# Linear attention with two expert layers on one core: norms first, transposes reordered, routing reordered

## The chip, the cores and the metric

One core of one Trainium2 chip. The time is that of the device for one execution, in microseconds (us). The kernel before was run three times: 834.59 us in the median, 834.49 to 839.33.

## What is computed

Attention with a positive feature map, then a top-1 mixture of eight experts, then a dense layer of three matmuls joined by max. All is f32, 2304 tokens of 512 features (4 batches of 576 tokens, 8 heads of 64).

```python
def phi(x):
    proj = np.einsum('bhsd,df->bhsf', x, w_phi)
    proj = proj - np.max(np.abs(proj), axis=-1, keepdims=True)
    return np.concatenate([np.exp(proj), np.exp(-proj)], axis=-1)
q_p, k_p = (phi(q), phi(k))
kv = np.einsum('bhsf,bhsd->bhfd', k_p, v)
z = np.sum(k_p, axis=2)
num = np.einsum('bhsf,bhfd->bhsd', q_p, kv)
den = np.einsum('bhsf,bhf->bhs', q_p, z)[..., None] + 1e-06

xn = x / (np.linalg.norm(x, axis=-1, keepdims=True) + 1e-06)
en = expert_emb / (np.linalg.norm(expert_emb, axis=-1, keepdims=True) + 1e-06)
logits = xn @ en.T / tau
expert_idx = np.argmax(logits, axis=1)
# out[token] = gate * relu(x @ w1[e]) @ w2[e], then max(x @ w1, x @ w2, x @ w3) @ w_out
```

## The kernel before

The order of all instructions is written out by hand; each engine runs its own list in order, and semaphores make it wait for the others. The attention part goes in rounds, `for r in range(R1)` with 18 rounds, numbered from 0. The keys are cut into 18 steps, the queries into 16 pieces that follow the keys by four and more rounds. A round does, in this order:

- `q_front`: the projection of a query piece on TensorE (tiles `psqf`), copied out by ScalarE (`pq`), and its largest magnitude over the partitions by a reduction on GpSimd (`mq`). `q_exp`: for the piece of the round before, the subtraction on VectorE (`pq<-pq,mq`) and two exponentials on ScalarE (`ex`).
- `k_proj(r + 1)`: the projection of the next key step on TensorE into two PSUM banks (`pskp`, j = 0 and 1), for each the largest magnitude (`mk`) and the subtraction (`pk`) on VectorE, and two exponentials on ScalarE (`kp`).
- `fin`, in rounds 5, 9 and 14 and after the loop: what is left to do for a finished batch (transposes `psz` and `pskv`, copies `zp` and `kvb` on VectorE).
- `xwork`: a finished piece of the attention's output x. In rounds 7, 9, 11, 13 and 16 a new piece is begun: transposes of the denominators (`psxd`), their reciprocals (`r`) and the raw logits (`lp`, `lraw`) on VectorE, the transpose of the numerators (`psx`), the scaling (`x`) on VectorE, its write to DRAM (`x_d`), and its sum of squares on ScalarE (`junk`). In the round after each of these the rest of its tiles follow.
- `k_T(r + 2)`: transposes of a later key step (`pskT`), copied by ScalarE (`kT`). `q_T`: transposes of a later query piece (`psqT`), copied by VectorE (`qT`).
- `k_acc`: accumulation of this round's keys and values (`kv`) and of the keys' sums (`z`) in banks of their own; `q_num` and `q_den`: numerators (`psn`, copied to `oT` by ScalarE) and, in every second of these rounds, denominators (`psd`, copied to `dn` by VectorE); `k_pair(r + 1)`: the sum of two key tiles on VectorE (`zr`), in whose place `z` of this round must have been read.

All the transposes and projections take their PSUM bank in turn from one pool of five (`bank`, tag "W"), so each waits until the reader of the tile allocated five earlier has finished.

`prep_experts` computes the norms of the expert embeddings: 8 rows of 512, a square and sum, then a chain of some twenty small operations on VectorE (`rsqrt`) and the scaling of `emb`; its second half transposes them (`ps_en`). The first half stands at the end of round 0, its VectorE part behind `zr` of that round. After the loop come the last numerators, the logits' argmax (`rt.argmax`) and the routing (`rt.blocks`, the generator `chain`): counts per expert (`inc`, `rt_n`), positions (`nb` to `tr`), one-hot groups (`R`) and the matmul that gives each block its token list (`rt_tok`, copied to `s2t`). Between its parts the last five tiles of x (13 to 17) are transposed, scaled and written; their sums of squares end ScalarE's list before the expert layer's weight casts. The expert layer begins with a gather of x by that list on GpSimd (`xs<-x_d,s2t`). Loads of keys, values and queries are issued from SyncE's queue, w_phi, embeddings and tau from ScalarE's.

Of the kernel before, what the change touches and what calls it, by code (L numbers as in the profile page):

```python
# [8 lines left out]
F32 = mybir.dt.float32  # L9
# [37 lines left out]
def attention(tc, q, k, v, w_phi, expert_emb, tau, x_d, lraw, ssq, ident, io, late, rt, ids):  # L47
# [19 lines left out]
    with ExitStack() as ctx:  # L67
# [60 lines left out]
        def load_kv(n):  # L128
            if n < len(loads):
                f, *a = loads[n]  # L130
                f(*a)

        w2 = cp.tile([P, NF], F32, tag="w2", name="w2")
        nc.scalar.dma_start(out=w2[0:D], in_=w_phi)
        load_kv(0)
        nc.scalar.dma_start(out=w2[D:P], in_=w_phi)
        emb = cp.tile([E, H * D], F32, tag="emb", name="emb")
        nc.scalar.dma_start(out=emb, in_=expert_emb)
        taub = cp.tile([E, 1], F32, tag="taub", name="taub")
        nc.scalar.dma_start(out=taub, in_=tau.rearrange("(a b) -> a b", b=1).to_broadcast([E, 1]))  # L140
        load_u(0, 1, (0,))
        load_q(0)
        load_u(0, 1, (1,))
        load_kv(2)
# [20 lines left out]
        rt.prep(QR)  # L165

        def prep_experts():
            sq = wk.tile([P, H * D], BF16, tag="junk", name="esq_junk", bufs=1)
            esq = cp.tile([E, 1], F32, tag="esq", name="esq")
            nc.scalar.activation(sq[0:E], emb, AF.Square, accum_out=esq)  # L170
            ern = cp.tile([E, 1], F32, tag="ern", name="ern")
            for _ in rsqrt(nc, cp, ern, esq, [E, 1], "e"):
                pass
            nc.vector.tensor_tensor(ern, ern, esq, op=ALU.mult)
            nc.vector.tensor_scalar(ern, ern, 1e-6, taub, op0=ALU.add, op1=ALU.mult)
            nc.vector.reciprocal(ern, ern)
            nc.vector.tensor_scalar(emb, emb, ern, None, op0=ALU.mult)
            yield
            ps = bank("ps_en")
            for p in range(NP_):  # L180
                nc.tensor.transpose(ps[:, p * E:(p + 1) * E], emb[:, p * P:(p + 1) * P], ident[:E, :E])
            psv = ps[:, 0:NP_ * E].rearrange("p (a e) -> p a e", e=E)
            nc.vector.tensor_copy(enp[0:D, :, 2:2 + E], psv[0:D])
            nc.vector.tensor_copy(enp[D:P, :, 2 + E:2 + 2 * E], psv[D:P])
            yield


        kT, kp, zr, kvs, acc = {}, {}, {}, {}, {}

        def k_T(n):  # L190

# [11 lines left out]
        def k_proj(n):  # L203
            if n >= NS:
                return
            psb = [bank(f"pskp{n}_{j}").rearrange("p (i f) -> p i f", f=NF) for j in range(2)]
            for i in range(4):
                for j in range(2):
                    x = slice(j * D, (j + 1) * D)
                    nc.tensor.matmul(psb[j][:, i, :], kT[n][x, i, :], w2[x], start=True, stop=True)  # L210
            o = kp[n] = wk.tile([P, 4, 2, 2 * NF], F32, tag="kp", name=f"kp{n}")
            for j in range(2):
                m = wk.tile([P, 4], F32, tag="mk", name=f"mk{n}_{j}")
                nc.vector.tensor_reduce(m, psb[j], axis=AX.X, op=ALU.max, apply_absolute_value=True)
                d = wk.tile([P, 4, NF], F32, tag="pk", name=f"pk{n}_{j}")
                nc.vector.tensor_tensor(d, psb[j], m.unsqueeze(2).to_broadcast([P, 4, NF]), op=ALU.subtract)
                nc.scalar.activation(o[:, :, j, 0:NF], d, AF.Exp)
                nc.scalar.activation(o[:, :, j, NF:], d, AF.Exp, scale=-1.0)


        def k_pair(n):
# [175 lines left out]
        def x_sq(t):  # L397
            junk = wk.tile([P, H * D], BF16, tag="junk", name=f"junk{t}", bufs=1)
            nc.scalar.activation(junk, xs.pop(t).rearrange("p h d -> p (h d)"), AF.Square, accum_out=ssq[:, t:t + 1])
# [52 lines left out]
                    yield  # L452

        R1 = back[NV - 4]
        k_T(0)
        k_T(1)
        k_proj(0)
        k_pair(0)
        pe = prep_experts()
        fin = None  # L460
        for r in range(R1):

# [5 lines left out]
                    q_exp(m * NP_ + 2 * g + pp)  # L468
            k_proj(r + 1)

            if fin is not None:
                for _ in fin:
                    pass
                fin = None
            if xwork:
                if next(xwork[0], "end") == "end":
                    xwork.pop(0)
                    if xwork:
                        next(xwork[0])
            k_T(r + 2)  # L480
            if r + LEAD + 1 in at:
                q_T(at[r + LEAD + 1])
            for _ in pe if r == 2 else ():
                pass

# [23 lines left out]
                    k_acc(*pc)  # L509
            k_pair(r + 1)  # L510
            if r == 0:
                next(pe)
            if r == 7:
                rt.token_ids(ids, QR)
            if r == R1 - 3:
# [21 lines left out]
        for p in range(2, NP_):  # L537
            q_num(m0 * NP_ + p)
        xa = [(t, rv, x_out(t)) for t, rv in ra]
        q_num((m0 + 1) * NP_)  # L540
        free = [("kv0", 512), ("kv1", 512), ("z", 256)]
        chain = rt.blocks(lambda nm: ps1.tile([P, free[0][1]], F32, tag=free.pop(0)[0], name=nm), bank)
        next(chain)
        x_put(*xa[0], act=True, dma=nc.scalar, sq=False)
        for p in range(1, NP_):
            q_num((m0 + 1) * NP_ + p)
            if p == 1:
                x_put(*xa[1], act=True, dma=nc.scalar, sq=False)
        xb = [(t, rv, x_out(t)) for t, rv in rb]
        x_put(*xb[0], act=True, dma=nc.scalar, sq=False)  # L550
        for x in xb[1:]:
# [1 line left out]
            x_put(*x, dma=nc.sync, sq=False)  # L553
        for _ in chain:
            pass
        for t in ta + tb:
            x_sq(t)


# [715 lines left out]
```

## Time and profile before

| | before |
|---|---|
| median of three runs (lowest to highest) | 834.59 us (834.49 to 839.33) |
| the profiled execution: its time, its span | 835.01 us, 833.2 us |
| TensorE busy, share of the span | 790.5 us, 95% |
| VectorE, ScalarE, GpSimd busy | 520.2, 453.4, 163.6 us |
| mean granted clock of TensorE | 0.969 |

The page of the profile gives for each engine its busy time. A stage in which TensorE is busy nearly throughout is bound by it; in one with pauses the rows in order of time tell what released each wait, in brackets: `[1.92 <-DVE pk L216]` means that the engine stood still 1.92 us until VectorE's instruction on line 216 had finished. PE is TensorE, DVE VectorE, ACT ScalarE, POOL GpSimd, SPq SyncE's DMA queue.

### The profile page before, as it was taken

What the parts mean: (1) busy time and instruction counts of PE and PEld (TensorE: products, weight loads), DVE (VectorE), ACT (ScalarE), POOL (GpSimd) and SP (SyncE); (2) the same over time, 40 slices, a digit from 0 to 9 for tenths busy, and PEclk for the clock granted to TensorE, in tenths of its full rate; (3) what the DMA queues carried; (4) which work ended last, traced back from release to release, by engine and by line L of the source; (5) the groups of instructions that cost most, each with busy time, mean ns of one, the idle gap of its engine ahead of it and who ended that gap; (6) DMA issues with size and microseconds to landing.
All of it is one profiled execution on the core that took longest, in us unless ns stands there. A gap on an engine that the chain in (4) does not pass through costs nothing. (4 is left out here: it accounts for less than half of the span.)

```text
span 833.2 us, 14145 instructions
## 1 busy us (share of the span) xinstructions
PE 790.5 (95%) x5617; PEld 661.5 (79%) x5617; DVE 520.2 (62%) x670; ACT 453.4 (54%) x632; POOL 163.6 (20%) x117
## 2 busy tenths in 40 slices
PE   7788988998989999999999999999999999999996
PEld 5655655575578888888888887999989999899984
DVE  5976567456779999989889897899312222122210
ACT  4576556476488888888888795544221112211111
POOL 1554224244052021011061102000121001200001
PEclk8899889789999999999999999999999999999999
DMA  8434323222334427641764542442021001200001
GB/s 208 109 81 105 78 66 83 55 77 79 143 127 147 153 97 285 250 139 43 258 235 176 190 160 103 157 160 102 26 76 52 1 1 39 76 1 1 0 26 52
DMA packets 61989, 87.82 MB, mean 105 GB/s; under 512 B 9488, under 2 KB 39832, under 8 KB 61920
## 3 DMA queue, kind: packets, MB, share of 16 engines
q1 hardware_dynamic: 53248, 64.25, 24.2%
q0 software_dynamic: 4880, 15.99, 5.9%
q10 hardware_dynamic: 3792, 6.64, 2.1%
q8 instruction: 46, 0.75, 0.4%
q14 instruction: 23, 0.19, 0.1%
HBM read 129.59 MB, written 16.00 MB: 175 GB/s over the span
## 5 line engine op out<-in xcount | busy, mean ns | idle before, releaser
L879 DVE TENSOR_TENSOR wL<-raw,wH 128x2048 fp32r<-128x2048 f32 x88 | 199.8, 2288 | 20.0 <-ACT wH L878 19.1
L878 ACT CAST wH<-raw 128x2048 fp32r<-128x2048 f32 x88 | 167.5, 1915 | 28.0 <-PE ph L905 13.7
L1106 PE MATMUL ps<-yH,m2WH 128*128 128x384 f32 x432 | 145.1, 336 | 1.3 <-ACTq L1242 1.3
L1106 PE MATMUL ps<-yH,m2WL 128*128 128x384 f32 x432 | 145.0, 336 | 0.0
L1106 PE MATMUL ps<-yL,m2WH 128*128 128x384 f32 x432 | 145.0, 336 | 0.0
L326 POOL PARTITION_ALL_REDUCE mq<-pq x32 | 70.5, 2252 | 122.3 <-ACT pq L324 122.3
L1106 PEld LDWEIGHTS ps<-yH,m2WH 128*128 128x128 f32 x432 | 81.2, 188 | 1.8 <-ACTq L1242 1.7
L1114 ACT CAST h2H<-mm 128x384 fp32r<-128x384 f32 x36 | 18.5, 514 | 115.6 <-DVE mm L1111 115.6
L1106 PEld LDWEIGHTS ps<-yL,m2WH 128*128 128x128 f32 x432 | 81.2, 188 | 0.1
L1106 PEld LDWEIGHTS ps<-yH,m2WL 128*128 128x128 f32 x432 | 81.2, 188 | 0.0
L849 POOL DMA_INDIRECT xs<-x_d,s2t x22 | 44.9, 2040 | 153.3 <-PE psxT L888 88.5
L1060 POOL DMA_INDIRECT yg<-ys,c2s x18 | 24.8, 1378 | 245.0 <-PE psyT L1075 220.2
L937 PE MATMUL py<-wH,hH 128*128 128x512 f32 x176 | 70.4, 400 | 0.4 <-ACT hH L923 0.4
L937 PE MATMUL py<-wH,hL 128*128 128x512 f32 x176 | 69.1, 393 | 0.3 <-DVE hL L924 0.3
L937 PE MATMUL py<-wL,hH 128*128 128x512 f32 x176 | 68.8, 391 | 0.0
L1110 DVE TENSOR_TENSOR mm<-mm,ps 128x384 f32<-128x384 f32 x36 | 19.9, 553 | 74.4 <-PE ps L1106 74.4
L905 PE MATMUL ph<-wH,xH 128*128 128x512 f32 x176 | 56.5, 402 | 0.7 <-ACT xH L891 0.7
L905 PE MATMUL ph<-wH,xL 128*128 128x512 f32 x176 | 54.8, 392 | 0.1
L905 PE MATMUL ph<-wL,xH 128*128 128x512 f32 x176 | 54.5, 391 | 0.0
L1111 DVE TENSOR_TENSOR mm<-mm,ps 128x384 f32<-128x384 f32 x36 | 20.0, 555 | 43.7 <-PE ps L1106 43.7
L1128 ACT ACTIVATE ot<-pso,gatec 128x512 f32<-128x512 f32 x18 | 12.4, 689 | 60.2 <-PE pso L1126 32.9
L1129 POOL DMA_INDIRECT out_dram<-ot,c2t x18 | 17.7, 983 | 132.3 <-ACT ot L1128 129.6
(214 smaller groups left out, 1446.7 us busy)
## 6 DMA issues: line engine op xcount, KB each, us to landing
raw<-in_moe_w_dram SPq DMA_DIRECT2D x88, 1024.0 KB
wr<-in_moe_w_dram SPq DMA_DIRECT2D x18, 512.0 KB
ys<-y ACTq DMA_DIRECT2D x22, 256.0 KB
q<-in_q_dram SPq DMA_DIRECT2D x8, 576.0 KB
kv<-in_v_dram SPq DMA_DIRECT2D x8, 512.0 KB
x_d<-x SPq DMA_DIRECT2D x15, 256.0 KB
kv<-in_k_dram SPq DMA_DIRECT2D x7, 512.0 KB
wr<-in_moe_w_out_dram SPq DMA_DIRECT2D x6, 512.0 KB
```

Of the source, the lines that this page charges most:

```text
L326: nc.gpsimd.partition_all_reduce(mx.rearrange("p a b -> p (a b)"), d.rearrange("p a b -> p (a b)"), P, ReduceOp.absmax)
L849: nc.gpsimd.indirect_dma_start(out=d, out_offset=None, in_=self.x_d, in_offset=bass.IndirectOffsetOnAxis(ap=self.s2t[:, j:j + 1], axis=0))
L878: nc.scalar.copy(wH, ex.raw[i])
L879: nc.vector.tensor_tensor(wL, ex.raw[i], wH.bitcast(F32), op=ALU.subtract)
L905: nc.tensor.matmul(ph[:, n * 512:(n + 1) * 512], a[:, cs], w[:, c * DF + n * 512:c * DF + (n + 1) * 512], start=(kc == 0 and f == 0), stop ...
L937: nc.tensor.matmul(py, a[:, cs], w[:, ws], start=(fc == 0 and q == 0), stop=(fc == 7 and q == 2))
L1060: self.nc.gpsimd.indirect_dma_start(out=d, out_offset=None, in_=self.ys[0:rows, :], in_offset=bass.IndirectOffsetOnAxis(ap=self.rt.c2s[:, ...
L1106: nc.tensor.matmul(ps, w[:, c], y[:, k], start=(k == 0 and q == 0), stop=(k == NK - 1 and q == 2))
L1110: nc.vector.tensor_tensor(m, m, pss[1], op=ALU.max)
L1111: nc.vector.tensor_tensor(m, m, pss[2], op=ALU.max)
L1114: nc.scalar.copy(hH[:, f], m)
L1129: nc.gpsimd.indirect_dma_start(out=self.out, out_offset=bass.IndirectOffsetOnAxis(ap=self.rt.c2t[:, t:t + 1], axis=0), in_=o, in_offset=None)
```

## The change

At the start: the embeddings are loaded ahead of w_phi on ScalarE's queue; the keys of the second unit are loaded ahead of the values of the first; the norms of the embeddings are taken on VectorE altogether (square and sum instead of ScalarE's) and stand ahead of the first key step. In round 0 the query transposes stand at the round's end. In the rounds: `k_proj` is cut into the projection and `k_exp`, the two halves of the key exponentials; `k_T` and `q_T` stand right behind the projection, `q_T`'s copies between the two halves, and `fin` and `xwork` behind all of these. At the end: the routing's first part stands ahead of the second query half's numerators, its second part ahead of the last three x tiles; tile 13 is scaled by VectorE instead of ScalarE; and the sums of squares of tiles 13 and 14 stand between the copies of numerators.

```diff
+        emb = cp.tile([E, H * D], F32, tag="emb", name="emb")
+        nc.scalar.dma_start(out=emb, in_=expert_emb)
         w2 = cp.tile([P, NF], F32, tag="w2", name="w2")
         nc.scalar.dma_start(out=w2[0:D], in_=w_phi)
-        load_kv(0)
         nc.scalar.dma_start(out=w2[D:P], in_=w_phi)
-        emb = cp.tile([E, H * D], F32, tag="emb", name="emb")
-        nc.scalar.dma_start(out=emb, in_=expert_emb)
...
+        load_u(0, 0, (0,))
         load_u(0, 1, (0,))
+        load_u(0, 0, (1,))
         load_q(0)
...
-            sq = wk.tile([P, H * D], BF16, tag="junk", name="esq_junk", bufs=1)
+            sq = wk.tile([P, H * D], F32, tag="x", name="esq_junk", bufs=5)
+            nc.vector.tensor_tensor(sq[0:E], emb, emb, op=ALU.mult)
             esq = cp.tile([E, 1], F32, tag="esq", name="esq")
-            nc.scalar.activation(sq[0:E], emb, AF.Square, accum_out=esq)
+            nc.vector.tensor_reduce(esq, sq[0:E], axis=AX.X, op=ALU.add)
...
+            kpb[n] = psb
+
+        def k_exp(n):
+
+            if n >= NS:
+                return
+            psb = kpb.pop(n)
             o = kp[n] = wk.tile([P, 4, 2, 2 * NF], F32, tag="kp", name=f"kp{n}")
             for j in range(2):
...
                 nc.scalar.activation(o[:, :, j, NF:], d, AF.Exp, scale=-1.0)
+                if j == 0:
+                    yield
...
+        pe = prep_experts()
+        next(pe)
         k_T(0)
         k_T(1)
         k_proj(0)
+        for _ in k_exp(0):
+            pass
         k_pair(0)
-        pe = prep_experts()
...
             k_proj(r + 1)
 
+            k_T(r + 2)
+            ke = k_exp(r + 1)
+            next(ke, None)
+            if r and r + LEAD + 1 in at:
+                q_T(at[r + LEAD + 1])
+            for _ in ke:
+                pass
             if fin is not None:
...
-            k_T(r + 2)
-            if r + LEAD + 1 in at:
-                q_T(at[r + LEAD + 1])
             for _ in pe if r == 2 else ():
...
             if r == 0:
-                next(pe)
+                q_T(at[LEAD + 1])
...
         xa = [(t, rv, x_out(t)) for t, rv in ra]
-        q_num((m0 + 1) * NP_)
         free = [("kv0", 512), ("kv1", 512), ("z", 256)]
         chain = rt.blocks(lambda nm: ps1.tile([P, free[0][1]], F32, tag=free.pop(0)[0], name=nm), bank)
         next(chain)
-        x_put(*xa[0], act=True, dma=nc.scalar, sq=False)
-        for p in range(1, NP_):
+        x_put(*xa[0], dma=nc.sync, sq=False)
+        x_put(*xa[1], act=True, dma=nc.scalar, sq=False)
+        for p in range(NP_):
             q_num((m0 + 1) * NP_ + p)
-            if p == 1:
-                x_put(*xa[1], act=True, dma=nc.scalar, sq=False)
+            if p < 2:
+                x_sq(ta[p])
+        next(chain)
...
-        for t in ta + tb:
+        for t in tb:
             x_sq(t)
```

What stands where, at three places. VectorE at the start, the kernel before: behind the second key tile come the query copies, the pair sum of round 0 and then the norms (`rs_` and `ern` are the tiles of the chain, `esq` the sums of squares).

```order
L308 COPY qT_237<-psqT_0_238 128x4x72
L308 COPY qT_237<-psqT_1_244 128x4x72
L225 TENSOR_TENSOR zr_273<-kp_215 128x1024
L36 TENSOR_SCALAR rs_ge<-esq 8x1
L37 TENSOR_SCALAR rs_ie<-rs_ge 8x1
L38 TENSOR_SCALAR ern<-rs_ie 8x1
```

The changed kernel, VectorE right behind the identity matrix:

```order
L28 TENSOR_SCALAR ident<-idn 32x32 x4
L170 TENSOR_TENSOR esq_junk<-emb 8x512
L172 TENSOR_REDUCE esq<-esq_junk 8x1
L36 TENSOR_SCALAR rs_ge<-esq 8x1
L37 TENSOR_SCALAR rs_ie<-rs_ge 8x1
L38 TENSOR_SCALAR ern<-rs_ie 8x1
```

The whole chain, with a square and a sum of its own, now stands ahead of the first `mk`, and nothing of it is left behind `zr`.

TensorE in round 7, behind the key projection, before:

```order
L377 MATMUL psxd_1064<-ident,dn_990 128x128 x2
L394 MATMUL psx_1074<-ident,oT_843 128x128 x4
L199 MATMUL pskT_1084<-ident,kv_0_588 128x128 x4
L306 MATMUL psqT_0_1092<-ident,q_651 128x72 x4
L306 MATMUL psqT_1_1098<-ident,q_651 128x72 x4
L253 MATMUL kv_0_699<-kp_906,kv_1_386 32x256 x16
```

and changed:

```order
L201 MATMUL pskT_1052<-ident,kv_0_589 128x128 x4
L317 MATMUL psqT_0_1067<-ident,q_646 128x72 x4
L317 MATMUL psqT_1_1073<-ident,q_646 128x72 x4
L388 MATMUL psxd_1085<-ident,dn_991 128x128 x2
L405 MATMUL psx_1095<-ident,oT_844 128x128 x4
L264 MATMUL kv_0_700<-kp_914,kv_1_387 32x256 x16
```

The transposes of x have moved from ahead of those of keys and queries to behind them; the accumulation `kv` stays last. VectorE in the same round, behind the subtractions of the queries, before:

```order
L214 TENSOR_REDUCE mk_0_1052<-pskp_0_1041 128x4
L216 TENSOR_TENSOR pk_0_1054<-pskp_0_1041,mk_0_1052 128x512
L214 TENSOR_REDUCE mk_1_1058<-pskp_1_1042 128x4
L216 TENSOR_TENSOR pk_1_1060<-pskp_1_1042,mk_1_1058 128x512
L380 TENSOR_SCALAR r_1067<-psxd_1064 128x16
L381 RECIPROCAL r_1067<-r_1067 128x16
L384 TENSOR_TENSOR lp_1070<-psxd_1064,r_1067 128x2x32 x2
L386 TENSOR_REDUCE lraw<-lp_1070 128x16
L407 TENSOR_TENSOR x_1079<-psx_1074,r_1067 128x512
L308 COPY qT_1091<-psqT_0_1092 128x4x72
L308 COPY qT_1091<-psqT_1_1098 128x4x72
```

and changed:

```order
L223 TENSOR_REDUCE mk_0_1060<-pskp_0_1042 128x4
L225 TENSOR_TENSOR pk_0_1062<-pskp_0_1042,mk_0_1060 128x512
L319 COPY qT_1066<-psqT_0_1067 128x4x72
L319 COPY qT_1066<-psqT_1_1073 128x4x72
L223 TENSOR_REDUCE mk_1_1079<-pskp_1_1043 128x4
L225 TENSOR_TENSOR pk_1_1081<-pskp_1_1043,mk_1_1079 128x512
L391 TENSOR_SCALAR r_1088<-psxd_1085 128x16
L392 RECIPROCAL r_1088<-r_1088 128x16
L395 TENSOR_TENSOR lp_1091<-psxd_1085,r_1088 128x2x32 x2
L397 TENSOR_REDUCE lraw<-lp_1091 128x16
L418 TENSOR_TENSOR x_1100<-psx_1095,r_1088 128x512
```

The two query copies have moved from the end to between the first and the second half of the keys.

ScalarE in the routing, from the first x tile that it scales there, before (tile 13, then 14):

```order
L405 ACTIVATE x_2736<-psx_2710,r_2665 128x64 x8
L408 DMA x_d<-x_2736 128x512
L354 COPY oT_2139<-psn_2746 128x288
L405 ACTIVATE x_2756<-psx_2715,r_2665 128x64 x8
L408 DMA x_d<-x_2756 128x512
L354 COPY oT_2139<-psn_2766 128x288
L354 COPY oT_2139<-psn_2776 128x288
L405 ACTIVATE x_2801<-psx_2786,r_2676 128x64 x8
L408 DMA x_d<-x_2801 128x512
L399 ACTIVATE junk_2879,ssq<-x_2736 128x512
L399 ACTIVATE junk_2881,ssq<-x_2756 128x512
```

and changed (tile 14 first):

```order
L416 ACTIVATE x_2730<-psx_2716,r_2666 128x64 x8
L419 DMA x_d<-x_2730 128x512
L365 COPY oT_2140<-psn_2740 128x288
L410 ACTIVATE junk_2750,ssq<-x_2727 128x512
L365 COPY oT_2140<-psn_2752 128x288
L410 ACTIVATE junk_2762,ssq<-x_2730 128x512
L365 COPY oT_2140<-psn_2764 128x288
L365 COPY oT_2140<-psn_2774 128x288
L416 ACTIVATE x_2828<-psx_2813,r_2677 128x64 x8
L419 DMA x_d<-x_2828 128x512
L410 ACTIVATE junk_2877,ssq<-x_2828 128x512
```

One scaling of eight pieces is gone from the list, and two of the five sums of squares (`junk`) stand between the copies; three are left at the end.

## Rows read from the trace of the kernel before

**Rows 1.** Stretches: us, busy us (instructions) of PE, PEld, DVE, ACT, POOL; clock, DMA share, GB/s.

```profile
56.00:211.00 155.00, 141.11 (x1804) 93.59 (x1796) 94.05 (x181) 94.71 (x207) 53.11 (x24) 0.89 0.29 80
260.00:520.00 260.00, 258.88 (x1277) 214.64 (x1275) 238.06 (x179) 215.26 (x175) 47.86 (x25) 1.00 0.50 177
```

**Rows 2.** In order of time, the start: start us, us, engine line op, [idle before <-releaser].

```profile
4.08 1.92 SPq L105 DMA_DIRECT2D q<-in_q_dram  x1
...
7.96 0.69 DVE L214 TENSOR_REDUCE mk<-pskp 128x4 f32<-128x512 f32 x1 [5.10 <-PE pskp L210]
...
16.36 0.61 ACT L218 ACTIVATE kp<-pk 128x512 f32<-128x512 f32 x1
...
18.89 1.25 PE L320 MATMUL psqf<-qT,w 64*128 64x144 f32 x16
19.11 1.23 DVE L225 TENSOR_TENSOR zr<-kp 128x1024 f32<-128x1024 f32 x1 [2.60 <-PE z L258]
```

**Rows 3.** In order of time, the norms' chain in round 1 and round 2's query projection.

```profile
20.26 0.13 DVE L36 TENSOR_SCALAR rs_ge<-esq 8x1 f32<-8x1 f32 x1
...
20.52 4.30 POOL L326 PARTITION_ALL_REDUCE mq<-pq  x2 [6.64 <-ACT pq L324]
...
20.78 1.04 DVE L40 TENSOR_TENSOR rs_te<-ern 8x1 f32<-8x1 f32 x1
...
25.75 0.67 DVE L214 TENSOR_REDUCE mk<-pskp 128x4 f32<-128x512 f32 x1
...
29.25 2.29 PE L320 MATMUL psqf<-qT,w 64*128 64x144 f32 x16 [4.57 <-DVE qT L308]
...
29.68 1.23 DVE L225 TENSOR_TENSOR zr<-kp 128x1024 f32<-128x1024 f32 x1 [0.48 <-ACT kp L218]
```

**Rows 4.** In order of time, round 4: the finished batch's sums.

```profile
52.81 1.02 PE L269 MATMUL z<-kvT,enp 128*32 128x256 f32 x8 [1.39 <-ACT kvT L265]
```

**Rows 5.** In order of time, round 7, in which a piece of x begins.

```profile
82.12 0.44 PE L306 MATMUL psqT<-ident,q 72*128 72x72 f32 x4 [1.92 <-DVE pk L216]
...
82.61 0.69 DVE L216 TENSOR_TENSOR pk<-pskp,mk 128x512 f32<-128x512 f32 x1
...
83.45 0.71 PE L306 MATMUL psqT<-ident,q 72*128 72x72 f32 x4 [0.88 <-DVE r L380]
...
84.09 3.64 PE L253 MATMUL kv<-kp,kv 128*32 128x256 f32 x32
...
85.00 0.81 DVE L308 COPY qT<-psqT 128x288 f32<-128x288 f32 x2
```

**Rows 6.** In order of time, the same places in rounds 5 and 16.

```profile
62.58 1.93 PE L253 MATMUL kv<-kp,kv 128*32 128x256 f32 x32
...
194.53 0.44 PE L306 MATMUL psqT<-ident,q 72*128 72x72 f32 x4 [2.11 <-DVE pk L216]
194.90 3.34 PE L253 MATMUL kv<-kp,kv 128*32 128x256 f32 x32
```

**Rows 7.** Stretches, columns as in rows 1: a pause and two stretches after pauses.

```profile
84.00:88.00 4.00, 4.00 (x42) 1.85 (x44) 1.78 (x5) 1.68 (x4) 0.00 (x0) 0.50 0.21 72
154.00:156.00 2.00, 0.93 (x13) 0.69 (x15) 1.83 (x6) 2.00 (x5) 2.00 (x2) 1.00 0.00 0
159.00:170.00 11.00, 11.00 (x97) 6.23 (x89) 2.89 (x4) 2.97 (x8) 1.72 (x1) 0.50 0.25 58
```

**Rows 8.** In order of time, the routing and the first gather.

```profile
223.79 0.17 DVE L671 TENSOR_SCALAR nb<-rt_n 128x8 f32<-128x8 f32 x1 [1.22 <-PE rt_n L665]
...
230.70 0.95 DVE L628 TENSOR_TENSOR R<-ir,trb 128x768 fp32r<-128x768 f32 x1
...
234.04 0.18 DVE L696 CAST s2t<-rt_tok 128x25 int32<-128x25 f32 x1 [0.28 <-PE rt_tok L685]
...
234.77 0.63 ACT L399 ACTIVATE junk<-x 128x512 bf16<-128x512 f32 x1
...
236.38 1.30 POOL L849 DMA_INDIRECT xs<-x_d,s2t  x1 [29.63 <-ACT junk L399]
```

More of the change, by code (lines that the diff above doesn't have):

```diff
@@ L185, in prep_experts @@
             yield
-        kT, kp, zr, kvs, acc = {}, {}, {}, {}, {}
+        kT, kp, kpb, zr, kvs, acc = {}, {}, {}, {}, {}, {}
         def k_T(n):
```

## The prediction

> **What bounds the kernel now.** I read the table of stretches first [rows 1]. From 260 to 520 us the reader should see TensorE busy 258.88 of 260 us at a granted clock of 1.00: this is the expert layer and the beginning of the dense one, which the change does not touch, and it starts when the routing hands it its first rows. So whatever the attention part and the routing gain or lose reaches the end almost 1:1. Between 56 and 211 us the same table shows TensorE busy 141.11 of 155 us and a clock of 0.89: there are pauses, and the clock is lowered. Here alone can the change act. So I read next the instructions in order of time, at three places: the first rounds [rows 2 to 4], a round in which a new piece of x is begun [rows 5], and the routing [rows 8]. In each, what matters is the releaser in brackets: it says what ended the wait.
>
> Durations are from the profiled execution: span 833.2 us, 835.0 us with what lies around it. The median of the three runs is 834.59, so I use 835.0 as the base and the difference of 0.4 is far below all terms.
>
> **The start.** Today VectorE runs the embeddings' norms in round 1, from 20.26 to 25.75 [rows 3], and only then reduces the keys' projection. The query copies come behind that, and TensorE waits 4.57 us for them until 29.25 [rows 3]. Moved ahead of the keys, the chain fills time in which VectorE waits: it sat idle 5.10 us before its first reduction at 7.96 [rows 2]. How long is it there? Of its 5.5 us two small operations on 8x1 took over 1 us (one stands in [rows 3], 1.04) where the one before took 0.13; they began while partition reductions ran on GpSimd (two from 20.52, 4.30 together). Without GpSimd I count 0.9 less for each: 3.7. To this come a square and a reduction over 8x512, which no row shows on VectorE; bounds are 0 and the 0.69 of the 128x512 reduction [rows 2]; I take 0.65 each, since its row has as many elements in a partition. Sum 5.0. It starts when the embeddings have landed. They now go first on ScalarE's queue, where w_phi went first, and the query load stood behind that until 4.08 [rows 2]. So 4.0 to 9.0, and the first key reduction comes at about 9.1 instead of 7.96: 1.1 late. If the embeddings land only at 6, it is 3 late.
>
> The Trainium skill (SBUF — State Buffer, Who interferes with whom) says that a VectorE operation with two SBUF inputs and a GpSimd operation that reads SBUF exclude one another until the first has finished. By that each of the two would have waited for up to a whole reduction of 2.15, the chain alone would be some 2.6 us shorter than I count and the start 1.1 us better than below, 837.3 in all; the row shows a wait of 0.9 and the sum goes by it.
>
> From the first reduction at 7.96 to the last exponential of the second key tile, 16.36 + 0.61 [rows 2], is 9.0 us of VectorE and ScalarE alone. From 9.1 that gives 18.1. Then the pair sum (1.23 [rows 2]) and the query copy, now behind it (0.81 [rows 5]), so round 1's first query projection starts at 20.1 instead of 18.89 [rows 2]. The reordered loads are hidden: the second key load needs only to be there by then. From 18.89 to the start of the pause (29.25 - 4.57 = 24.7) TensorE needs 5.8 us. Round 2 therefore starts at 25.9 instead of 29.25: **3.3 us gained**.
>
> Some of it is given back at once. The pair sum waits for ScalarE's exponentials of the second half of the keys; today the query copy (0.81) lies between and only 0.48 of wait is left [rows 3]. With the copy moved ahead, nothing lies between: 0.81 more in each of the rounds 1 and 2, where VectorE is what TensorE waits for, and about 0.3 in round 4, where ScalarE's copy of the sums ends a wait of 1.39 [rows 4]. 3.3 - 1.6 - 0.3 = **1.4 us gained** at the end of round 4; bounds 0 and 3.3.
>
> **The x rounds.** There are five rotating PSUM banks, and a transpose takes the bank used five allocations earlier. Counting them after the two banks of the key projection: today the x pieces and the key transpose take the three free banks, and the two query transposes wait for the projection's banks. That is what [rows 5] show: the first at 82.12 released by pk, the second at 83.45, just after the last pk (82.61 + 0.69 = 83.30). After the change key and query transposes take the free banks, and the x transposes (in rounds 5, 9, 14 first those of the finished sums) wait for the same two. The wait is not removed; it changes its owner. The accumulation behind it (84.09) is still held until the last pk, and this pk is now later by the query copies put ahead of it, 0.81 [rows 5]. What lies between release and accumulation is the same: one transposition group. **0.8 us lost** in rounds 5, 7, 11 and 13 each (in round 5 the accumulation stands at 62.58 now [rows 6]), and between 0 and 0.8 in 9 and 14, where two groups more stand behind the wait in either order; I take 0.5. In rounds 10, 12 and 16 only the first pk is needed, which does not move; round 16 shows it (194.53 [rows 6]): nothing. Sum 4 x 0.8 + 2 x 0.5 = 4.2; bounds 2.1 and 5.
>
> **The routing.** The first gather stands at 236.38, 1.0 after ScalarE's last sum of squares (234.77 + 0.63), while its index list was ready at 234.04 + 0.18 [rows 8]. Five such sums end the stage; two now go between the copies, where ScalarE waits anyway, and one ScalarE scaling goes to VectorE. Three remain. The list comes about 0.4 earlier, since the count no longer stands behind a numerator (nb on VectorE at 223.79 [rows 8]). The last x tile is scaled about 1 us later, behind one more one-hot group (0.95 us [rows 8]), so its sum of squares and its write come later too. The gather then comes **1.1 us** earlier; bounds 0.3 and 1.5.
>
> **The clock.** In the rows TensorE's clock falls to 0.50 after pauses: 0.50 at 84 to 88 after the pauses of 1.92 and 0.88 in [rows 5]; and after 154 to 156, where it is busy 0.93 of 2 us, 0.50 for 11 us [rows 7]. Its price is in one pair of rows: the 32 accumulations of a round took 1.93 at 62.58 [rows 6] and 3.64 at 84.09 [rows 5], so 1.7 more. The x rounds' pauses get longer (in round 7 1.92 + 0.88 today, 0.8 more then), and rounds 4, 5 and 14, which have short ones, get pauses near 2. I count one more fall: 1.7 lost; bounds 0 and five falls.
>
> Sum: 835.0 - 1.4 + 4.2 - 1.1 + 1.7 = **838.4 us**, 0.4% slower, which is within what can be told: I take 1% as what a measurement of this kernel distinguishes from no change (its three runs lie between 834.49 and 839.33).
>
> **The rivals.** (A) Faster: a lowered clock ends at a moment of its own, so accumulation that starts later runs less of its time at half speed, and each 0.8 costs 0.4; no new fall comes, and the start keeps its whole 3.3. For it speaks that TensorE is busy all of 84 to 88 and of 159 to 170 while the clock stays low [rows 7]: work alone does not at once end it. 835.0 - 3.3 + 2.1 - 1.1 = 832.7. The Trainium skill (TensorE: Matmul & The Clock Gate, The HAM clock gate) says that the clock is set by a monitor that runs on without regard to the kernel's start; by that rule this rival's first condition holds. If also the 11 us at 0.50 in [rows 7] did not come back, 5 or 6 us more would go: 827. (B) Slower by over 1%: five more falls of the clock, one each in rounds 4, 5, 7, 11, 14. 835.0 - 1.4 + 4.2 - 1.1 + 5 x 1.7 = 845.2. It decides from a pause of 1.9 us on (1.92 in [rows 5], 2.11 in [rows 6], both followed by accumulations of 3.3 to 3.6 us), while the 1.39 in [rows 4] is followed by no fall in the rounds I read; I reckon the new pauses at 1.85. (C) The start gains nothing, because the embeddings land late: 838.4 + 1.4 = 839.8, inside the likeliest case's own range.
>
> **How the numbers follow.** Likeliest case with (C) 0.52, its own range 835 to 842.5; (A) 0.29, of it 0.10 for the 827, whose spread of a few us puts 0.07 below 826.2; (B) 0.17; the rest lies beyond. The range leaves out the far ends of (A) and (B): 829.5 to 845.5. Faster by over 1% (below 826.2) needs that far end of (A): 0.07. Slower by over 1% (above 842.9) is (B) nearly whole: 0.15. Within 1%: 0.78.
>
> **What would show it.** In the profile after: the first key reduction near 9.1 and round 2's query projection near 25.9, without a wait for the query copies; in round 7 the x transposes, not the query's, released by pk, and the accumulation 0.8 later after the last denominator copy than today; two sums of squares between the last output copies and the gather 1.1 earlier after the end of round 17. I am wrong if the accumulations in the x rounds start as early as today or earlier, if the lowered stretches are fewer than today's, or if the first reduction comes later than 11.

## The result, and the profile after

The changed kernel takes 823.84 us in the median (822.45 to 825.75) beside 834.54 (833.85 to 839.33) before: ratio 0.9865, 95% interval 0.9828 to 0.9901. A second comparison gave 823.23 and a ratio of 0.9838 (0.9755 to 0.9922). By the first that is 1.3% faster, by its interval 1.0 to 1.7%; the forecast was 838.4, 0.4% slower, from 829.5 to 845.5.

The profiled execution has a span of 821.5 us (823.43 us in all) and a mean granted clock of 0.986, against 833.2 and 0.969. Its stretches, with the columns of [rows 1]:

```profile
56.00:211.00 155.00, 140.65 (x1958) 92.72 (x1946) 104.60 (x215) 99.88 (x221) 53.11 (x24) 0.98 0.32 90
260.00:520.00 260.00, 256.97 (x1277) 214.84 (x1276) 233.62 (x173) 210.41 (x174) 44.43 (x24) 1.00 0.49 171
```

In the first stretch TensorE is busy as long as in [rows 1], but gets through 154 more matmuls, and the clock column says 0.98 instead of 0.89 (1.00 is the full 2.4 GHz, 0.50 the lower of its two levels, 1.2 GHz). To see where the time went I cut the span at four landmarks: the first query projection (`psqf`) of round 5, the first denominators (`psd`) behind the loop, the first matmul of the expert layer (`ph`), the end.

| us | before | after | difference | forecast |
|---|---|---|---|---|
| start to round 5 | 56.48 | 56.83 | +0.35 | -1.4 |
| round 5 to the end of the rounds | 155.27 | 143.25 | -12.02 | +4.2 and +1.7 |
| routing, to the first `ph` | 29.82 | 28.69 | -1.13 | -1.1 |
| expert and dense layers | 591.63 | 592.73 | +1.10 | 0 |

All of the gain, and all of the error, lies in the second line. The two rows for it, the kernel before and then the changed one:

```profile
56.48:211.75 155.27, 141.38 (x1802) 94.10 (x1798) 94.32 (x182) 94.71 (x207) 53.11 (x24) 0.89 0.29 82
```

```profile
56.83:200.08 143.25, 129.59 (x1801) 87.16 (x1797) 94.16 (x182) 94.33 (x207) 53.11 (x24) 0.98 0.32 88
```

The same 1,801 or so matmuls, 11.8 us less of busy TensorE: the pauses in it are as long in sum as before (13.7 us, and 13.9 before). What changed most is how fast it ran between them. Round 7 of the changed kernel, in order of time (columns as in [rows 5], which answer to it):

```profile
81.56 0.69 DVE L225 TENSOR_TENSOR pk<-pskp,mk 128x512 f32<-128x512 f32 x1
...
82.12 0.57 ACT L203 COPY kT<-pskT 128x512 f32<-128x512 f32 x1
...
82.40 0.41 PE L388 MATMUL psxd<-ident,dn 128*128 128x128 f32 x2 [2.07 <-DVE pk L225]
82.74 0.66 PE L405 MATMUL psx<-ident,oT 128*128 128x128 f32 x4
...
83.33 1.93 PE L264 MATMUL kv<-kp,kv 128*32 128x256 f32 x32
...
83.61 0.69 DVE L225 TENSOR_TENSOR pk<-pskp,mk 128x512 f32<-128x512 f32 x1
```

There is one pause instead of two. `psxd` waits for the first `pk` (81.56 + 0.69), as forecast; but `psx` does not wait for the last `pk`: it runs at 82.74, before that one even starts at 83.61. It comes just behind the end of ScalarE's key copy, 82.12 + 0.57 = 82.69. So the accumulation comes 6.57 us after the round's first query projection (83.33 - 76.76) instead of 7.60 (84.09 in [rows 5], less 76.49), 1.0 earlier where I had forecast 0.8 later; and its 32 matmuls take 1.93 us, not 3.64. The clock, in the stretches of [rows 7] and in two that are low now:

```profile
84.00:88.00 4.00, 4.00 (x70) 2.25 (x64) 3.90 (x10) 2.46 (x6) 0.00 (x0) 1.00 0.18 68
126.00:128.00 2.00, 1.87 (x10) 1.21 (x14) 1.97 (x5) 1.53 (x4) 1.01 (x1) 0.50 0.00 0
...
159.00:170.00 11.00, 9.97 (x135) 7.31 (x134) 8.78 (x20) 8.30 (x21) 4.15 (x3) 1.00 0.41 141
184.00:186.00 2.00, 2.00 (x24) 0.99 (x20) 1.90 (x7) 1.15 (x2) 0.00 (x0) 0.50 0.03 8
```

Rounds 7, 9, 11, 13 and 16 were each followed by a stretch at 0.50 before; now only 11 and 16 are, and the second profile of the changed kernel (after_again, below) shows the same two. I call lost clock the time in a stretch times one less the granted clock: added up over stretches of 1 us it is 17.1 us in the rounds of before and 3.4 in those of after.

The start (the rows that answer to [rows 2] and [rows 3]):

```profile
2.89 0.68 DVE L170 TENSOR_TENSOR esq_junk<-emb 8x512 f32<-8x512 f32 x1
...
8.08 0.20 DVE L177 TENSOR_SCALAR ern<-ern,taub 8x1 f32<-8x1 f32 x1 [0.92 <-DMA taub<-in_moe_tau_dram]
...
8.90 0.67 DVE L223 TENSOR_REDUCE mk<-pskp 128x4 f32<-128x512 f32 x1
...
20.03 2.29 PE L331 MATMUL psqf<-qT,w 64*128 64x144 f32 x16 [3.52 <-DVE qT L319]
...
27.13 1.25 PE L331 MATMUL psqf<-qT,w 64*128 64x144 f32 x16
...
33.65 0.54 PE L183 MATMUL ps_en<-ident,emb 8*128 8x8 f32 x4 [2.58 <-DVE pk L225]
34.12 3.38 PE L264 MATMUL kv<-kp,kv 128*32 128x256 f32 x32
...
37.86 1.25 PE L331 MATMUL psqf<-qT,w 64*128 64x144 f32 x16
...
46.76 1.16 PE L212 MATMUL pskp<-w,kT 64*128 64x128 f32 x14 [0.98 <-ACT pq L335]
```

The chain ends where forecast (first key reduction 9.1 forecast, 8.90 measured; round 1's query projection 20.1 and 20.03), but that projection then runs at the low clock, 2.29 us instead of the 1.25 in [rows 2], and round 2 starts at 27.13, not 25.9. The last four rows show where the rest of the lead goes. In round 2 the transposes of the embeddings (`ps_en`) wait 2.58 us for `pk`. The accumulation behind them still starts 1.27 earlier than before, but takes 3.38 at the low clock, and round 3 begins at 37.86 instead of 37.69. Before, the same accumulation ran at full speed:

```profile
35.39 1.93 PE L253 MATMUL kv<-kp,kv 128*32 128x256 f32 x32
```

In round 4, which begins at 43.97 instead of 45.12, the key projection waits 0.98 for ScalarE's copy of the query projection (`pq`), for which it did not wait before; by its end the lead is gone. The same wait of 0.98 stands in after_fill (below), where the clock is at 1.00 in this round, so the clock does not make it.

The routing (the rows that answer to [rows 8]):

```profile
220.87 0.16 DVE L715 CAST s2t<-rt_tok 128x25 int32<-128x25 f32 x1
...
221.35 0.63 ACT L410 ACTIVATE junk<-x 128x512 bf16<-128x512 f32 x1
...
223.52 1.30 POOL L868 DMA_INDIRECT xs<-x_d,s2t  x1 [28.44 <-issue]
```

The gather stands 23.44 after the end of the rounds (223.52 - 200.08) instead of 24.63: 1.2 earlier, 1.1 forecast. In the expert layer 1.1 is given back. Up to 454 us TensorE keeps its lead there of 12.8 us; from 461.60 on the lead is 11.5 to 11.7. What lies between is a weight cast (`wH`) that waits 2.06 for its load, where before the same cast waited 0.80 for TensorE, and behind it, by the same 1.3 late, the activation `h`, for which the transposes `pshT` wait. The kernel before, then the changed one:

```profile
460.45 1.91 ACT L878 CAST wH<-raw 128x2048 fp32r<-128x2048 f32 x1 [0.80 <-PE py L937]
...
473.10 1.09 PE L919 MATMUL pshT<-ident,h 128*128 128x128 f32 x8
```

```profile
448.94 1.91 ACT L897 CAST wH<-raw 128x2048 fp32r<-128x2048 f32 x1 [2.06 <-DMA raw<-in_moe_w_dram]
...
461.60 1.09 PE L938 MATMUL pshT<-ident,h 128*128 128x128 f32 x8 [1.24 <-ACT h L931]
```

The changed kernel's second profile shows both waits too (2.11 and 1.28). No run tests why the load is late there.

### The profile page after: what moved, and what is told of

Read it like the earlier page. It is cut to its first block, busy times and chain, and to the rows that moved or that the text cites. A ratio compares the mean times of both kernels' runs of the same rounds, so it can differ in the third digit from the quotient of the medians.

```text
span 821.5 us, 14129 instructions
## 1 busy us (share of the span) xinstructions
PE 780.2 (95%) x5617; PEld 655.3 (80%) x5617; DVE 520.5 (63%) x673; ACT 450.2 (55%) x622; POOL 162.6 (20%) x117
## 3 DMA queue, kind: packets, MB, share of 16 engines
q10 hardware_dynamic: 3648, 6.38, 2.1%
## 5 line engine op out<-in xcount | busy, mean ns | idle before, releaser
L868 POOL DMA_INDIRECT xs<-x_d,s2t x22 | 42.3, 1923 | 153.5 <-PE psxT L907 90.1
```

The costliest lines, as they stand in the source:

```text
L868: nc.gpsimd.indirect_dma_start(out=d, out_offset=None, in_=self.x_d, in_offset=bass.IndirectOffsetOnAxis(ap=self.s2t[:, j:j + 1], axis=0))
```

## The experiments

Two theories stood against each other. **The banks** (theory 1 in the expectations): my step on the x rounds failed because the five PSUM banks are not handed out in turn, and what helped is that nothing waits for the last `pk`. **The clock** (theory 5): what helped is that TensorE's clock falls less often; the wait itself is small. Each kernel was compared with runs of before on its own chip; before had medians of 834.5 to 838.2 us there.

| kernel | median us | ratio to before (95%) |
|---|---|---|
| changed | 823.84 | 0.9865 (0.9828 to 0.9901) |
| rounds_only | 828.2 | 0.9914 (0.9877 to 0.995) |
| start_tail | 834.5 | 0.9962 (0.9935 to 0.9989) |
| after_strict | 840.03 | 1.0068 (1.0028 to 1.0108) |
| strict_fill | 823.9 | 0.9838 (0.9756 to 0.992) |
| before_fill2 | 825.26 | 0.9849 (0.9766 to 0.9933) |
| after_fill | 816.4 | 0.9753 (0.9673 to 0.9834) |
| kT_early | 829.85 | 0.9928 (0.9891 to 0.9964) |
| after_late_q | 822.9 | 0.986 (0.9784 to 0.9937) |
| rounds_fill | 823.54 | 0.9875 (0.9794 to 0.9956) |
| fill_11_16 | 822.13 | 0.9799 (0.9752 to 0.9845) |

**Which part: rounds_only and start_tail.** The first is the kernel before with `k_exp` cut out of `k_proj` and `k_T`, `q_T` ahead of `fin` and `xwork`; the second is the changed kernel with the rounds of before.

> The rounds' part of the change alone; start and tail as before. Theory 1 (the gain is in the x rounds, through the banks): in the changed kernel's trace rounds 7 to 14 end 12.2 us earlier than before relative to round 5, and the start gives nothing, so 834.5 - 12 = 822 to 824, with the x transposes of round 7 not held by the last pk. Rival 2 (start and tail hold part of it: the trace shows the gather 1.1 earlier after the end of the rounds): 826 or more. Rival 3 (my forecast for the rounds, a loss of 4.2, holds and the gain needs the start's other phase): 836 to 839.

> The start's and the routing's part of the change alone; the rounds as before. Theory 1: the start gives at most 0.3 by round 5 and the routing 1.1, of which the expert layer gives some back, so 833 to 834.5. Rival 2 (start and tail hold part of the gain, or the earlier start shifts the clock's falls): 830 or less. My forecast's own terms for these parts, -1.4 and -1.1: 832.

The ratios multiply to 0.9876, the whole change has 0.9865: the parts add up. In the profile of rounds_only the stretch from round 5 takes 143.23 us, as in the changed kernel (143.25), without the new start and the new routing; in that of start_tail it takes 156.13 (155.27 before), and its routing 28.68, as in the changed kernel (28.69). So the gain of the rounds is the rounds' own. But start and tail are worth something as well, 0.4% in the ratio, so the first theory's "nothing" was too little.

**The step that failed: after_strict.** The changed kernel, with the banks taken strictly in turn, which I had taken for granted.

```diff
+        turn = [0]
+
         def bank(name):
-            return ps1.tile([P, 512], F32, tag="W", name=name, bufs=5)
+            turn[0] += 1
+            return ps1.tile([P, 512], F32, tag=f"W{turn[0] % 5}", name=name)
```

> The changed kernel with the five PSUM banks handed out in strict turn, which the prediction had taken for granted; nothing else. Theory 1 (what failed is that step): now the x transposes of round 7 get the bank of the key projection's second half and wait for the last pk; the accumulation stands about 0.8 later than in the changed kernel, the second pause is back, the clock falls in rounds 7, 9 and 13 again, and the time goes back by 8 to 14 us, to 832 to 838. Rival 4 (the order on TensorE alone, keys and queries ahead of x, made the gain, whatever the bank): stays at 822 to 826. Half way (wait back, no fall of the clock): 826 to 829.

It takes 840.03 us, close to the 838.4 of the prediction, above the 832 to 838 expected, and is slower than before. Round 7:

```profile
83.89 0.41 PE L391 MATMUL psxd<-ident,dn 128*128 128x128 f32 x2 [2.07 <-DVE pk L228]
...
85.11 0.69 DVE L228 TENSOR_TENSOR pk<-pskp,mk 128x512 f32<-128x512 f32 x1
...
85.94 1.09 PE L408 MATMUL psx<-ident,oT 128*128 128x128 f32 x4 [1.65 <-DVE r L394]
...
86.96 2.93 PE L267 MATMUL kv<-kp,kv 128*32 128x256 f32 x32
```

Now `psx` does start just behind the last `pk` (85.80; the view names the instruction after it), the second pause is back, and the accumulation stands 8.71 after the round's start (86.96 - 78.25): 1.1 later than before, where I had said 0.8. The rounds take

```profile
57.43:218.42 160.99, 140.49 (x1802) 93.93 (x1798) 95.10 (x182) 94.83 (x207) 53.11 (x24) 0.89 0.28 78
```

which is 5.7 more than before; the forecast's two terms for them were 4.2 + 1.7 = 5.9. The forecast was that of another kernel. In the one that was built, the bank that a tile takes depends on when its last reader is done in the program's own order: the key copy `kT` now stands on ScalarE ahead of the key exponentials, so its bank is free before that of the projection's second half, and `psx` gets it. The list of banks in the built program says so: `psx` of round 7 shares its bank with `pskT`, and in after_strict with the second `pskp`. In the kernel before it is the second `psqT` that shares the bank of the second `pskp`.

**The two costs apart: before_fill2, after_fill, strict_fill.** Matmuls of no use, two instructions of 0.12 us a call, fill the pauses in three kernels. They write to the half of the bank of `z` that nobody reads.

```diff
+        def fill(key):
+            for _ in range(fl.pop(key, 0)):
+                nc.tensor.matmul(zl[0][:, 256:256 + P], rt.ones, rt.ones, start=len(zl) > 1, stop=True, skip_group_check=True)
...
         def x_log(ts):
...
+            fill("xd")
```

`zl` holds one tile throughout, so `start` is always false; a table gives the calls for each place and round. (A first version, before_fill, had `start=True` and twice the calls: 826.37 us, with the sums in z spoilt, and its times are not used.)

> The kernel before, with matmuls of no use on TensorE (128x128, 0.12 us each at full clock, some 16 to 21 in each of rounds 7, 9, 11, 16, 7 in round 13, into an unused half of a bank) in the pauses that stand ahead of the clock's falls. Banks and waits stay as they are. Theory 5 (the clock carries the gain): low stretches between 82 and 200 us lost 17.0 us of clock before; if they go, 834.5 - 10 to 15 = 820 to 825. Rival 6 (the waits carry it, the clock falls whenever it likes): 833 to 836.

> The kernel before, with matmuls of no use on TensorE in its pauses (each call two instructions of 0.12 us at full clock; 2 to 9 calls a pause, in rounds 2, 4, 7, 9, 11, 13 and 16), written so that the sums in z are kept (the run named before_fill had spoilt them, and had twice as many). Banks and waits as before. Theory 5 (the clock carries the gain): the lost clock of rounds 7 to 16, 17.0 us, goes nearly whole, 834.5 to 820 or less, as fast as the changed kernel or faster. Theory 1 (the wait for the last pk carries it): 832 to 836.

> The changed kernel with the same useless matmuls in its pauses (rounds 1, 2, 4, 5, 7, 9, 11, 13, 14, 16). Theory 5: the changed kernel still loses 10.3 us of clock in its profile, of which 1.7 lie in the routing and 1.7 ahead of round 1: 823.8 - 5 to 7 = 817 to 819. If the waits that the change took away are worth something of their own, it is faster than the kernel before with the same matmuls by as much: 1 to 4 us. Theory 1 alone: 823 to 825.

> The changed kernel with the banks in strict turn (waits for the last pk in rounds 5, 7, 9, 11, 13 and 14, some 1.4 to 1.65 us each) and useless matmuls in those pauses. This takes the two costs of the wait apart, beside the run named after_fill. Theory 5: the clock stays up, what is left is the waits' own length, at most 6 x 1.5 = 9, less what was hidden: 819 to 826. Theory 1 with the clock's falls no more than a side effect: 832 to 838.

Round 7 of before_fill2: the useless matmuls lie in the first pause of [rows 5], both waits end as before, and the accumulation takes 1.93 us where [rows 5] have 3.64.

```profile
82.36 1.95 PE L81 MATMUL z<-onesq 128*128 128x128 f32 x16
84.44 0.44 PE L320 MATMUL psqT<-ident,q 72*128 72x72 f32 x4
...
85.77 0.44 PE L320 MATMUL psqT<-ident,q 72*128 72x72 f32 x4 [0.16 <-DVE r L395]
86.14 1.93 PE L262 MATMUL kv<-kp,kv 128*32 128x256 f32 x32
```

From round 5 to the end of the rounds, before_fill2, after_fill and strict_fill:

```profile
58.80:201.10 142.30, 137.95 (x1899) 98.38 (x1895) 94.22 (x182) 94.40 (x207) 53.08 (x24) 1.00 0.32 89
```

```profile
54.03:194.31 140.28, 136.61 (x1889) 96.20 (x1885) 93.98 (x182) 94.03 (x207) 53.09 (x24) 1.00 0.33 89
```

```profile
55.06:202.40 147.34, 143.09 (x1956) 103.81 (x1952) 94.53 (x182) 94.41 (x207) 53.08 (x24) 1.00 0.31 86
```

| rounds, us | as built | clock kept up | lost by the clock |
|---|---|---|---|
| before | 155.27 | 142.30 | 13.0 |
| changed | 143.25 | 140.28 | 3.0 |
| changed, banks in turn | 160.99 | 147.34 | 13.7 |

Each figure is from one profile. With the clock at 1.00 in both, before and after differ by 2.0 us: so much are the shorter waits worth. The other 10.0 of the 12.0 are the clock's. (As built, the pauses add up alike, 13.9 and 13.7 us, since work at the low clock fills a part of the waiting. With the clock up, pauses and useless matmuls together are 16.3 us in before_fill2 and 14.4 in after_fill.) Of the forecast's own kernel the waits cost 5.0 more than before (147.34 - 142.30), at the upper of the bounds of 2.1 and 5 that I had given for them.

So both theories hold in part. after_strict and the changed kernel differ in the banks alone, and with the turn of the banks the second pause and the falls of the clock come back together, and in all ten of its executions the mean clock is lower (0.958 to 0.971) than in the changed kernel's eight (0.979 to 0.988): the bank does both. That it is the second pause which lets the clock fall is argued, not shown: in kT_early below it is gone from round 7, and the clock falls there all the same.

strict_fill (823.9) lies where theory 5 had it, after_fill just below. before_fill2, at 825.26, lies in neither range (820 or less, 832 to 836). Its whole time fell less than its rounds, because its clock fell in the routing instead (0.53 from 220 to 231), and there the 40 warming matmuls ahead of the first `psxT` became the bound: 7.38 us, and `psxT` 6.2 us behind the gather instead of 3.9.

after_fill, at 816.4 us (816.01 to 816.61), beats both kernels.

**Which edit frees the bank: kT_early and after_late_q.** The kernel before with only the key transposes moved ahead of the key exponentials; and the changed kernel with the query transposes behind both halves of them.

```diff
...
+            k_T(r + 2)
+            ke = k_exp(r + 1)
+            for _ in ke:
+                pass
             if fin is not None:
...
-            k_T(r + 2)
             if r + LEAD + 1 in at:
```

> The kernel before with one edit in the rounds: the key transposes and their ScalarE copy stand right behind the key projection, ahead of the key exponentials; query transposes, finished sums and x stay in the order of before. Theory 7 (the early key copy frees its bank before the last pk does, and the next transpose takes that bank): in round 7 the second query transpose takes the bank of the key transpose, not that of the key projection's second half; no second pause, the accumulation no later than 0.3 after the first pk's release and its transposes; most of the gain of the rounds, 822 to 828. Rival 8 (the x transposes behind keys and queries are what counts): 833 to 838.

> The changed kernel with the query transposes behind both halves of the key exponentials instead of between them. Theory 7: x still takes the bank of the early key copy, no wait for the last pk comes, and the last pk is 0.8 earlier, which nothing waits for: 822 to 826. Rival 9 (the query copies between the halves carry a part, by coming earlier): 827 or more.

Round 7 of kT_early has one pause, and both query transposes run through:

```profile
88.38 0.81 PE L315 MATMUL psqT<-ident,q 72*128 72x72 f32 x8 [1.92 <-DVE pk L223]
89.12 3.40 PE L262 MATMUL kv<-kp,kv 128*32 128x256 f32 x32
```

So the early key copy is what frees the bank, and the accumulation comes 6.38 after the round's start (89.12 - 82.74). But the clock fell there in this execution, the slowest of ten; the ten spread from 825.0 to 836.4, with the median at 829.85, so that the forecast of 822 to 828 was missed. Against before this one edit has a ratio of 0.9928, and all of the rounds' edits together (rounds_only) 0.9914; the intervals overlap, so whether the rest of the order adds anything cannot be told. In after_late_q (822.9) the place of the query copies makes no difference that can be told.

**The price of start and routing: rounds_fill.** rounds_only with the useless matmuls.

> The rounds' part of the change alone, with useless matmuls in its pauses as in the run named after_fill, and the start and routing of before. This gives the price of the start and the routing with TensorE's clock kept up, beside after_fill at 816.4. My terms for them: 1.4 to 3.3 in the start and 1.1 in the routing, so 819 to 821, round 5's query projection at 55.5 to 57.5 (54.03 in after_fill). If the start gives nothing even with the clock up: 817.5, round 5 at 54.

It takes 823.54 against 816.4 of after_fill: 7.1 us, where my terms gave 2.5 to 4.4. Round 5's query projection is at 58.35 instead of 54.03, so the start is worth 4.3 here, of which its lost clock (3.4 against 1.7) may be 1.7; the rounds are alike (140.3 in both); the routing takes 31.53 instead of 28.63, of which 1.2 is the earlier gather and the rest again the warming matmuls at the low clock (7.46 us against 6.33). With the clock up, round 2 of after_fill starts at 25.83; 25.9 was forecast.

**Does a fall that is kept off stay off: fill_11_16.**

> The changed kernel with the useless matmuls in rounds 11 and 16 alone, where both its profiles show a fall of the clock behind a pause of 2.09 and 2.29 us (1.7 us of lost clock each). Theory 5 (a fall that is kept off saves what it lost): these two falls go, the rest stays, 823.5 - 3.4 = 820, between 819 and 821.5, and a mean clock up by 0.004. Rival 10 (the clock falls somewhere else instead, and only filling all pauses helps): 822.5 to 824.

Not always. Three executions take 819.4, 819.7 and 819.7 us, as theory 5 says; three take 824.5, 824.5 and 826.3, longer than even rival 10 had it, at a mean clock of 0.976 to 0.979 instead of 0.986 to 0.990. The profile is of the second kind. Rounds 11 and 16 hold (last two rows). But the clock fell at 53, behind the pause of 1.43 at the end of round 4, and again in rounds 7 and 9, behind pauses of 2.07 and 2.26. The changed kernel's two profiles have the same pauses (1.42, 2.07, 2.26) at the same places and no fall behind them.

```profile
53.00:63.00 10.00, 10.00 (x86) 6.39 (x85) 3.35 (x5) 2.79 (x7) 2.25 (x2) 0.51 0.01 2
86.00:90.00 4.00, 4.00 (x45) 2.03 (x48) 2.62 (x9) 2.23 (x5) 0.00 (x0) 0.58 0.11 42
107.00:111.00 4.00, 3.46 (x20) 3.31 (x24) 3.96 (x13) 3.59 (x7) 0.00 (x0) 0.57 0.02 4
131.00:135.00 4.00, 3.79 (x58) 2.34 (x62) 3.86 (x12) 2.77 (x7) 1.09 (x1) 1.00 0.01 3
187.00:191.00 4.00, 4.00 (x74) 2.24 (x72) 3.86 (x10) 2.47 (x7) 0.38 (x1) 1.00 0.02 4
```

**The changed kernel once more: after_again.**

> The changed kernel once more, beside the three that follow. In the first profiles the product of span and mean granted clock is about the same for before and after (833.2 x 0.969 = 807, 821.5 x 0.986 = 810). Theory 5 (the gain is the clock's): again 822 to 826, and the product near 810 in each execution. Theory 1 would need a smaller product after than before.

It took 821.6 to 825.25 us, at clocks of 0.987 to 0.979; span times clock is 806 to 809, a little less than the 810 of the first profile. Of before, 19 executions on one chip (beside rounds_only; two of over 840 us left out) lie between 827.9 us (span 826.1, clock 0.980) and 840.0 (838.2, 0.965), and their span times clock between 807.7 and 812.9. So what sets apart two executions of the kernel before is for the most part the lost clock. Of the changed kernels' executions this holds less well: in fill_11_16 the product itself goes from 802.9 to 809.7. Beside after_again, before has 809.0 to 810.8; in the first profiles it was the other way round (807 before, 810 after). Within the few us that the product is good for, the two kernels cannot be told apart by work and waits, and the lost clock is what differs.

## Why the prediction was wrong

- **The start, -1.4.** The working of the chain was right: 9.1, 20.1 and 25.9 forecast, 8.90 and 20.03 measured, and 25.83 where the clock is kept up. That the first of them fits so well is in part luck: the norms began at 2.89 instead of 4.0 and then waited 0.92 for `taub`. By round 5 nothing was left (+0.35), for two reasons that the term did not have. One is the clock: round 1's projection and round 2's accumulation ran at 0.50. The other is a wait: in round 4 the key projection waits 0.98 for ScalarE, with the clock up too, and I had counted 0.3 for that round. In the kernels with filled pauses the start is worth 4.3, of which up to 1.7 is clock again; the rest is within my bounds of 0 and 3.3.
- **The x rounds, +4.2: the step that failed.** "There are five rotating PSUM banks, and a transpose takes the bank used five allocations earlier." The description of the kernel before says the same, and as a rule it is false. I checked it against [rows 5], where it holds, since there the free banks happened to come in that order. I then used it for an order of instructions in which a bank comes free out of turn. after_strict shows that the working behind the step was sound: with banks in turn the rounds lose 5.7. In the changed kernel the waits are 2.0 shorter, not 4.2 longer: the accumulation of round 7 comes 1.0 earlier, which I had named as a sign of being wrong. That the change moved the key copy ahead of the exponentials on ScalarE stood in the diff, and I read it only for what it does on TensorE.
- **The clock, +1.7.** I counted falls from the length of the new pauses and so had their sign from the failed step. It is the largest term of all: 10.0 us less instead of 1.7 more. The price of a fall was too low as well: 1.7 is what 32 accumulations lose (3.64 and 1.93), but the low stretch can go on behind them. From one query projection to the next, before against before_fill2, the falls cost 2.9 in round 7, 2.0 in 9, 1.6 in 11, 4.7 in 13 and the round behind it, and 1.7 in 16. The three that went, in 7, 9 and 13, make 9.6 of the 10.0. The far end of rival A (no new fall, the 11 us at 0.50 gone, start kept), at 827, came nearest, since it lets the clock gain; I gave it 0.10. But it had no reason for the falls to go, and 2.1 of longer waits.
- **The routing, -1.1.** The size was right: 1.13 to the first `ph`, 1.2 to the gather. The path was not, so part of this is luck. Counted from the end of the rounds, the list is ready 1.5 earlier (0.4 forecast) and ScalarE's last sum of squares ends 1.8 earlier, but the gather now stands 1.54 behind that sum instead of 0.98. What it waits for there the row does not name (`<-issue`); the landing of the last write of x is likely, but not shown.
- **What comes after reaches the end 1:1.** Nearly: 1.1 of 12.8 was given back in the expert layer.

The Trainium skill (TensorE: Matmul & The Clock Gate, The HAM clock gate) holds that the monitor behind the clock runs on without regard to the kernel, and that the same kernel therefore meets it differently from run to run. The six executions of fill_11_16 agree: one program, with mean clocks from 0.976 to 0.990. In which rounds the clock fell only the profiled one shows. What I failed to draw from it is that a single profile's falls are no sure basis for counting.

## What to carry to other kernels

Before you reason from a buffer pool's turn, look up which buffer each tile really gets in the built program, in both versions: moving a reader earlier can hand its buffer to someone who had been waiting for another. Where TensorE pauses for some 2 us again and again, look at the granted clock first: here it weighed five times as much as the waits, and cheap matmuls of no use in the pauses (after_fill) were worth 7 us on top of the change. Multiply span by mean clock for a first look at whether two kernels, or two executions, differ in work and waits or in the clock; it is good to a few us here (807.7 to 812.9 for one kernel), no better.

## What the runs showed that I had not expected

- The kernel before took from 827.9 to 840.0 us on one chip, with the product of span and clock between 807.7 and 812.9; the three runs that I had as its times (834.49 to 839.33) showed little of it.
- The pause does not decide alone. 2.07 and 2.26 us in rounds 7 and 9 were followed by no fall in the changed kernel's two profiles, and by one each in that of fill_11_16, which does the same in these rounds; 2.09 and 2.29 in rounds 11 and 16 by one each in both of the changed kernel's; and 1.43 in round 4 of fill_11_16 by 10 us at the low clock. So the pause of 1.9 us from which rival B was to decide is no border. What else decides, no run here shows.
- Matmuls with `start=True` into one half of a bank spoilt the sums that were being gathered in the other half; with `start=False` they did not. This is seen in two kernels that also differ in the number of calls.
